# Projections by position block, a resident u D, fewer loads and a new stage order in a fused attention and state-space kernel

## The chip, the cores and the metric

The kernel runs on one core of a Trainium2 chip, in one launch. The metric is the device time of a run in microseconds (us), median of the runs shown. The engines are TensorE (PE; its weight loads, PEld, are listed apart), VectorE (DVE), ScalarE (ACT), GpSimd (POOL) and SyncE (SP); SPq, ACTq, POOLq are their sequencers, which issue DMAs. A profile of one execution shows what each engine did and what it waited for.

## The reference

Two unrelated layers of one sequence of 2048 positions and 640 channels each, side by side in the output:

```python
# part A: sliding local dilated attention; H = 32, Dh = 20, W = 8, dil = 2
qkv = (x @ wqkv).reshape(B, S, 3, H, Dh)            # q, k, v by head
idx = pos[:, None] - 2 * arange(8)[None, :]         # 8 keys: 0, 2, .., 14 positions back
logits = einsum("bhsd,bhswd->bhsw", q, k[idx]) * Dh ** -0.5    # below position 0: -1e9
o = einsum("bhsw,bhswd->bhsd", softmax(logits), v[idx])
a = o @ wo
# part B: a diagonal state-space layer as a long convolution; N = 192
dt = exp(log_dt);  l = arange(2048) rounded to bf16
K = einsum("dn,dnl,dn->dl", C, exp(dt * A * l), dt * B).real   # A, B, C complex, 640 x 192
y = irfft(rfft(pad(u)) * rfft(pad(K)))[:L] + u * Dskip
out = concatenate([a, y], -1)                        # [1, 2048, 1280], bf16
```

## The kernel before, in words

**Part B** works through the channels in five chunks (`NCH` = 5, 128 channels each, c = 0 to 4). The table of the kernel K comes from powers of exp(dt A): `partB_prep` turns the parameters over with matmuls (`flip`, L175) so that the states lie on partitions; `gens` (L234) makes 11 powers with sines and stores them to DRAM (`Gdram`; chunks 0 and 1 in one batch, `gens0`, chunks 2 to 4 in another, `gens2`). For each chunk `Tables` loads them and builds by complex products on VectorE an X table of 20 entries (`xtab`) and a Y table of 33 entries (`ypos`, `yneg`; L264 to L269 and L313). `kgen` (L335) contracts them over the states on TensorE, in four pieces q of 128 small matmuls (L350, L355); each piece ends with a copy to `Kd` (L357), and a shift of `Kd` by DMA from GpSimd's queue follows (L360). Only one Y table is in memory at a time, and two X tables.

The convolution is a two-stage Fourier transform as matmuls: `spread` (L364) brings K into order, `f1` (L386) is the first stage, for u (`first_u`) or K, `f2` (L397) the second. `swap_halves` (L415) makes a copy with the halves exchanged by DMA, `product` (L420) does the complex product in place with four VectorE multiplications of 128x2048 (L422, L423, twice each), `ia` (L426) is the first stage back and its result Z is stored to DRAM for chunks 0 to 2 (`Zdram`) and kept for 3 and 4 (`Z34`). `inverse` (L787) is the second stage back (`last00` to `last03` for chunks 0 to 2, `last10` to `last13` for 3 and 4, each a quarter of l0). It loads a quarter of `Zdram` as `zq` (one buffer) and of the transposed u as `uq`, multiplies `uq` by Dskip on VectorE (L796), adds it with an identity matmul (L800), adds the transform (L803), and stores 4 pieces (L806).

**Part A** loads x transposed (`load`, 20 transposing DMAs on SP, L453) and projects it, 15 calls of `proj` (L465) over 5 tiles of 128 columns for each of k, q, v: four position blocks of 512 by 5 matmuls of 128x512, with a copy to `st` (two buffers, L472), and one store of 128 rows of 4 KB to DRAM (`qd`, `kd`, `vd`). Then four position blocks b of 512 go through `fetch` (q and k tiles by 10 loads), `logits` (L515: 10 VectorE products of 128x2048, L524, and 40 matmuls, exponential and normalisation, L528 to L542), `fetch_v` (20 loads), `av` (L544: 10 more products, L554, and 160 matmuls, L560) and `out_proj` (L566).

**The order.** Every stage runs under `at(name)`, which sets a priority from the place of that name in the list `ORDER`; a scheduler in the build then picks by it among the instructions that its own time simulation says are ready, and fixes one order for each engine and queue. Apart from that list (L138 to L144) the loop over c in the body says what stands in which pool. The tables' pool is released when the last `kgen` has run, and `HB` (the 4 MB matrix of the last stage, four loads of 1 MB) and `Z34` come in its place. The tail is made of the `last` stages.

Of the kernel before, what the change touches and what calls it, by code (L numbers as in the profile page):

```python
# [10 lines left out]
A = mybir.AluOpType  # L11
# [6 lines left out]
NCH = 5  # L18
# [120 lines left out]
k4 am2 inv4 v0 weights k0 u1 spec2 am0 q3 tab2 tab4 v3 prep load taby2 ypos1 ypos0 out1 xtab2 xtab0 tab1 tab0 q2 q1 swap1 k1 yneg1 load2 v2  # L139
mag2 u0 yneg0 fetch0 v4 q0 spread0 k2 tab3 mag0 kgen2 mag1 gens0 kgen4 last13 q4 fetch1 spec1 inv0 kgen1 kgen0 u2 ypos2 gens2 v1 prod4 taby3  # L140
yneg2 kgen3 k3 taby4 spec3 spec0 taby1 fetch2 ypos3 yneg4 spread3 inv3 logits0 swap0 xtab1 last10 xtab3 u3 inv2 spread1 taby0 u av3 av0
fetchv0 swap2 last12 av2 out0 prod1 inv1 yneg3 prod2 logits3 spec xtab4 mag4 last03 u4 fetchv1 ypos4 last11 last02 last01 swap3 mag3 out3
fetchv3 prod3 spec4 fetchv2 spread2 fetch3 av1 swap4 spread4 prod0 last00 out2 logits1 logits2 hb
# [4 lines left out]
def partB_prep(tc, pools, prm, Gd):  # L148
# [5 lines left out]
    nat = [pp.tile([128, NCH, CW], bf16, name="nat", tag="nat", bufs=5) for _ in range(6)]  # L154
    ldt = pp.tile([128, NCH], bf16, name="ldt")
    lsrc = prm["B_log_dt"].rearrange("(g c t) -> g t c", g=4, c=NCH, t=32)
    eng = [nc.sync, nc.scalar]
    for g in range(4):
        eng[g % 2].dma_start(out=ldt[32 * g:32 * g + 32, :], in_=lsrc[g])
    for a, nm in enumerate(["B_A_re", "B_A_im", "B_C_re", "B_C_im", "B_B_re", "B_B_im"]):  # L160
        src = prm[nm].rearrange("(g c t) n -> g t c n", g=4, c=NCH, t=32)
        for g in range(4):
            (eng[g % 2] if a < 2 else nc.gpsimd).dma_start(out=nat[a][32 * g:32 * g + 32], in_=src[g])
# [11 lines left out]
    def flip(a, diag):  # L175
        psb = [psp.tile([128, 512], f32, name="ps_tr", tag="b", bufs=4) for _ in range(2)]
        for c in range(NCH):
            rhs = dg[:, c, :] if diag else ident[:]
            for h in range(2):
                hs = slice(64 * h, 64 * h + 64)  # L180
                col = c * CW + 64 * h
                nc.tensor.matmul(psb[col // 512][:, col % 512:col % 512 + 64], lhsT=nat[a][:, c, 0:128], rhs=rhs[:, hs], start=True, stop=True, skip_group_check=True)
# [397 lines left out]
def kernel(  # L580
# [71 lines left out]
    with at("prep"):  # L652
        ta, wi, weights = partB_prep(tc, pools, prm, Gd)
# [200 lines left out]
```

## Time and profile before

| what | us |
|---|---|
| median of 3 runs | 465.58 (461.92 to 467.53) |
| the profiled execution's own time | 465.34 |
| its span, first to last instruction | 468.0 |
| TensorE busy | 341.5 |
| VectorE busy | 309.3 |
| ScalarE busy | 260.9 |
| GpSimd busy | 36.7 |

The span is the time from the first to the last instruction of the profiled execution. Busy times are sums over an engine's instructions. The profile's other parts: 40 slices of the span with a digit for the busy share in tenths; the chain of work that ended last, followed back from the last instruction; groups of instructions with their idle time before them and who ended it. A row of a window lists the window, its length, the busy time (and count) of PE, PEld, DVE, ACT and POOL, the granted clock of TensorE, the busy share of the DMA engines and GB/s. A row of waits gives who waited for whom, the sum in us, how often, and the longest.

| product c | first start of L422, us |
|---|---|
| 0 | 206.4 |
| 1 | 272.1 |
| 2 | 327.7 |
| 3 | 382.6 |
| 4 | 411.1 |

### The profile page before, as it was taken

What the parts mean: (1) busy time and instruction counts of PE and PEld (TensorE: products, weight loads), DVE (VectorE), ACT (ScalarE), POOL (GpSimd) and SP (SyncE); (2) the same over time, 40 slices, a digit from 0 to 9 for tenths busy, and PEclk for the clock granted to TensorE, in tenths of its full rate; (3) what the DMA queues carried; (4) which work ended last, traced back from release to release, by engine and by line L of the source; (5) the groups of instructions that cost most, each with busy time, mean ns of one, the idle gap of its engine ahead of it and who ended that gap; (6) DMA issues with size and microseconds to landing.
All of it is one profiled execution on the core that took longest, in us unless ns stands there. A gap on an engine that the chain in (4) does not pass through costs nothing.

```text
span 468.0 us, 13264 instructions
## 1 busy us (share of the span) xinstructions
PE 341.5 (73%) x5672; PEld 214.7 (46%) x5684; DVE 309.3 (66%) x448; ACT 260.9 (56%) x570; POOL 36.7 (8%) x80
## 2 busy tenths in 40 slices
PE   0558986999498783639488657899866789967654
PEld 0223432644146352427354446546454556645453
DVE  0576999987799477999029996099911679392101
ACT  1768543997672396624058743288322986936322
POOL 6830000003000200000020000200001000000000
PEclk9956898989898697666769869579985998989876
DMA  7999999345877684103824206143375934205966
GB/s 236 210 210 192 289 243 272 104 154 171 272 255 255 152 241 112 29 19 77 243 53 124 71 23 178 55 120 85 106 207 166 368 94 121 74 1 158 219 157 110
DMA packets 90378, 72.86 MB, mean 156 GB/s; under 512 B 44528, under 2 KB 82656, under 8 KB 88656
## 3 DMA queue, kind: packets, MB, share of 16 engines
q1 hardware_dynamic: 83920, 64.43, 51.2%
q0 software_dynamic: 2352, 5.18, 4.1%
q10 hardware_dynamic: 4048, 2.41, 2.3%
q8 instruction: 44, 0.72, 0.7%
q14 instruction: 14, 0.11, 0.1%
HBM read 38.93 MB, written 24.71 MB: 136 GB/s over the span
## 4 chain that ended last, share of the span: by engine, by line
PE 38%; DVE 20%; DMA 16%; issue 12%; ACT 8%; SPq 4%; ACTq 0%; DVEq 0%; POOL 0%; POOLq 0%
PE ps_p L471 10%; PE ps_k L355 6%; PE ps_k L350 6%; PE ps_ia L435 4%; DVE prod L524 4%; DVE p L554 4%; DMA Gdram<-cs 4%; DMA zq<-Zdram 3%; PE ps_ib L803 3%; SPq L453 3%; DMA kd<-st 2%; DVE krtmp L265 2%; ACT mag L307 2%; ACT Sp L412 2%; DMA Xg<-Gdram 2%
## 5 line engine op out<-in xcount | busy, mean ns | idle before, releaser
L471 PE MATMUL ps_p<-xT,w 128*128 128x512 bf16 x288 | 80.2, 421 | 24.3 <-ACT st L472 15.8
L471 PEld LDWEIGHTS <-w 128*128 128x128 bf16 x300 | 30.1, 105 | 63.0 <-issue 33.9
L524 DVE TENSOR_TENSOR prod<-qb,kb 128x2048 bf16<-128x2048 bf16 x40 | 47.3, 1217 | 7.1 <-PE ps_l L528 6.0
L472 ACT CAST st<-ps_p 128x512 bf16<-128x512 f32 x60 | 34.2, 585 | 31.7 <-PE ps_p L471 23.3
L554 DVE TENSOR_TENSOR p<-vb,attn 128x2048 bf16<-128x2048 bf16 x40 | 47.1, 1217 | 2.1 <-PE ps_o L560 2.0
L408 PE MATMUL ps_f<-A,cT 64*128 64x128 bf16 (+1 forms) x768 | 36.4, 230 | 16.3 <-ACT Sp L412 8.6
L394 ACT CAST A<-ps_f 128x512 bf16<-128x512 f32 x80 | 42.1, 614 | 8.3 <-PE ps_f L393 8.1
L412 ACT CAST Sp<-ps_f 128x512 bf16<-128x512 f32 (+1 forms) x96 | 42.8, 579 | 6.0 <-PE ps_f L408 5.9
L355 PE MATMUL ps_k<-Ytab,Xtab 64*20 64x33 bf16 x1280 | 28.3, 244 | 20.2 <-issue 20.2
L408 PEld LDWEIGHTS <-cT 64*128 64x128 bf16 x768 | 31.0, 105 | 25.5 <-issue 24.7
L357 ACT CAST Kd<-ps_k 128x264 bf16<-128x264 f32 x20 | 7.5, 379 | 61.7 <-PE ps_k L355 61.7
L796 DVE TENSOR_TENSOR uq<-uq,Dsb 128x1536 bf16<-128x1536 bf16 (+1 forms) x8 | 6.6, 825 | 50.7 <-DMA uq<-Udram 37.4
L560 PE MATMUL ps_o<-p,cHs 64*32 64x256 bf16 x640 | 31.2, 308 | 11.4 <-DVE p L554 10.1
L436 ACT CAST Z<-ps_ia 128x512 bf16<-128x512 f32 x40 | 21.6, 594 | 29.6 <-PE ps_ia L435 29.5
L355 PEld LDWEIGHTS <-Xtab 64*20 64x20 bf16 x1280 | 22.3, 124 | 26.3 <-issue 24.3
L350 PE MATMUL ps_k<-Ytab,Xtab 128*20 128x33 bf16 x1280 | 28.1, 249 | 5.4 <-issue 5.4
L435 PE MATMUL ps_ia<-cE,Sp 128*128 128x128 bf16 x160 | 23.7, 244 | 9.7 <-DVE Sp L423 9.7
L350 PEld LDWEIGHTS <-Xtab 128*20 128x20 bf16 x1280 | 22.6, 128 | 12.8 <-issue 11.2
L573 PE MATMUL ps_op<-wo,oT 128*128 128x320 bf16 x160 | 27.9, 321 | 0.0
L307 ACT ACTIVATE mag<-ta 128x192 bf16<-128x192 f32 x80 | 21.7, 353 | 10.4 <-DVE Ytab L313 10.4
L264 DVE TENSOR_TENSOR Ytab<-Ytab 128x384 bf16<-128x384 bf16 (+2 forms) x15 | 13.3, 888 | 21.4 <-DMA Ytab<-Gdram 21.1
L528 PE MATMUL ps_l<-prod,cGs 128*32 128x512 bf16 x160 | 24.7, 420 | 3.2 <-DVE prod L524 3.0
(101 smaller groups left out, 600.6 us busy)
## 6 DMA issues: line engine op xcount, KB each, us to landing
vb<-vd SPq DMA_DIRECT2D x80, 65.5 KB, 2.3
UT<-Sp SPq DMA_DIRECT2D x10, 512.0 KB, 7.3
HB<-k_HB SPq DMA_DIRECT2D x4, 1024.0 KB, 8.7
Gdram<-cs SPq DMA_DIRECT2D x11, 288.0 KB, 3.2
Xg<-Gdram SPq DMA_DIRECT2D x4, 768.0 KB, 7.1
Zdram<-Z SPq DMA_DIRECT2D x3, 1024.0 KB, 9.5
zq<-Zdram SPq DMA_DIRECT2D x12, 256.0 KB, 4.8
kb<-kd SPq DMA_DIRECT2D x20, 131.5 KB, 2.7
```

Of the source, the lines that this page charges most:

```text
L307: pin(self.nc.scalar.activation(out=self.mg[b // 8][:, b % 8], in_=ta[:, s], func=ACT.Exp, scale=-16.0 * (b + 1)))
L350: MM(o, lhsT=X[:, :, part, col], rhs=Y[:, :, part, col], start=False, stop=False, tile_position=(0, 32 * g), skip_group_check=True)
L355: MM(o, lhsT=X[hb:hb + 64, :, part - 2, col], rhs=Y[hb:hb + 64, :, part - 2, col], start=False, stop=(part == 3), tile_position=(hb, 32 * ...
L394: nc.scalar.copy(out=A1[:].rearrange("p k r s t -> p (k r) s t")[:, :, sig, 8 * q:8 * q + 8], in_=ps[:])
L408: nc.tensor.matmul(ps[h][:, kk], lhsT=C["T"][hs, k, 64 * (1 - r):64 * (1 - r) + 128], rhs=A1[hs, k, r, s0:s1, :].rearrange("p s t -> p (s ...
L412: nc.scalar.copy(out=o, in_=ps[h][:].rearrange("p k (s t) -> p s t k", t=64))
L435: nc.tensor.matmul(ps[:, i], lhsT=X[:, h, 4 * t:4 * t + 4, :].rearrange("p g k -> p (g k)"), rhs=C["E"][:, n_, :], start=(i == 0 and n_ == ...
L471: nc.tensor.matmul(ps[:], lhsT=self.w[which][:, kt, 128 * ct:128 * ct + 128], rhs=self.xT[:, kt, 512 * sc:512 * sc + 512], start=(kt == 0) ...
L472: nc.scalar.copy(out=st[:, sc], in_=ps[:])
L524: V.tensor_tensor(out=pr[:], in0=q[ct][:].unsqueeze(1).to_broadcast([128, 4, PB]), in1=windows(k[ct][:, 8 - 8 * wg:8 - 8 * wg + PB], 2, 4) ...
L554: V.tensor_tensor(out=p2[:], in0=windows(self.v[b][t][:, 2 * qp:2 * qp + 2, 0:PH], 2, 4), in1=at[:].unsqueeze(2).to_broadcast([128, 4, 2, ...
L560: nc.tensor.matmul(ps[half][32 * q:32 * q + 32, t % 2], lhsT=C["Hs"][r], rhs=p2[r, m, q2, :], start=(t % 2 == 0 and m == 0), stop=(m == 3) ...
```

## The change

- **Start.** The parameters are loaded with the channel as j p (128 partitions in a run) by one DMA each, all on SP, in an order written out; so are the w matrices and the Gdram stores of `gens0`, which were on the ScalarE and GpSimd queues. The flips then need 32-column pieces: 240 matmuls in place of 120. Five transposes of x are in the list of loads, and the other 15 are issued behind the stores of the powers (`then`, two or one behind each). Buffers of cs: 6 for 4, of nat: 6 for 5.
- **Projections.** `proj(which, sc)` does one position block of 512 for all five column tiles; the store has 128 partitions of five pieces of 1 KB. The 12 calls are ordered by block. q and k share one DRAM tensor `qkd`, so that `fetch` needs 5 loads of 128x2x526 a block in place of 10.
- **Loads of v.** Two tiles of 8 and 12 rows in place of five of 4: 8 loads a block in place of 20.
- **kgen in pieces.** The four pieces have four names in the order.
- **u D resident.** The whole transposed u is loaded once (2.5 MB, one DMA of SP) behind the last kgen, multiplied by Dskip in five VectorE multiplications, and kept. HB's loads move to GpSimd's queue.
- **Tail.** Chunks 0 to 2 go in eighths of l0, with two half buffers for z: 32 stores of 32x8x96 in place of 16 of 32x16x96, 24 loads of 128 KB in place of 12 of 256 KB.
- **A new `ORDER`** with the new names.

```diff
-    for a, nm in enumerate(["B_A_re", "B_A_im", "B_C_re", "B_C_im", "B_B_re", "B_B_im"]):
-        src = prm[nm].rearrange("(g c t) n -> g t c n", g=4, c=NCH, t=32)
-        for g in range(4):
-            (eng[g % 2] if a < 2 else nc.gpsimd).dma_start(out=nat[a][32 * g:32 * g + 32], in_=src[g])
+        def par(nm, t):
+            nc.sync.dma_start(out=t[:], in_=prm[nm].rearrange("(j p) n -> p j n", p=128))
...
+        for m in range(4 * NCH):
+            g, c, j, r = m // NCH, m % NCH, m // 4, slice(32 * (m % 4), 32 * (m % 4) + 32)
+            rhs = (dg[:, j, :] if diag else ident[:])[:, r]
+            for n0, n1, p, col in ((0, 128, slice(0, 128), c * CW + 32 * g), (128, 192, slice(64 * (g // 2), 64 * (g // 2) + 64), c * CW + 128 + 32 * (g % 2))):
+                nc.tensor.matmul(psb[col // 512][p, col % 512:col % 512 + 32], lhsT=nat[a][:, j, n0:n1], rhs=rhs, start=True, stop=True,
+                                 tile_position=(0, p.start), skip_group_check=True)
...
-        (nc.sync if ca else nc.scalar).dma_start(out=Gd[...], in_=cs.rearrange("p c r n -> p c (r n)"))
+        o = nc.sync.dma_start(out=Gd[...], in_=cs.rearrange("p c r n -> p c (r n)"))
+        then(o)
...
+    def then(store):
+        with at("load"):
+            for _ in range(2 if len(xs) > 8 else 1):
+                if xs:
+                    ins = a.load_x(xs.pop(0))
+                    tc.add_manual_dep(ins.ins, store.ins.name, ..., reason="order of the transfers")
...
-    def proj(self, which, ct):
-        st = self.pools["xw"].tile([128, 4, 512], bf16, name="st", tag="st", bufs=2)
-        for sc in range(4):
+    def proj(self, which, sc):
+        st = self.pools["xw"].tile([128, 5, 512], bf16, name="st", tag="st", bufs=2)
+        for ct in range(5):
...
+            nc.sync.dma_start(out=self.qkd[:, :, "qk".index(which), s], in_=st[:])
...
+            t = p.tile([128, 2, HALO + PB], bf16, name="qk", tag="qk", bufs=3)
+            nc.sync.dma_start(out=t[:], in_=self.qkd[:, ct, :, i0:i0 + PB + HALO])
...
+        for i, (d0, n) in enumerate(((0, 8), (8, 12))):
+            v = p.tile([128, n, PH + 6], bf16, name="vb", tag=f"vb{i}", bufs=1)
...
+        for q in range(4):
+            with at(f"kgen{self.c}{q}"):
+                self.kgen_part(q, Kd)
...
-            nc.sync.dma_start(out=HB[...], in_=hsrc[:, 16 * q:16 * q + 16])
+            nc.gpsimd.dma_start(out=HB[...], in_=hsrc[:, 16 * q:16 * q + 16])
+    with at("ud"):
+        nc.sync.dma_start(out=uD[:].rearrange("p x l t -> p (x l t)"), in_=Ud[:].rearrange("p x l t -> p (x l t)"))
+    for x in range(0, 2 * NCH, 2):
+        with at(f"ud{x // 2}"):
+            dv = ...
+            V.tensor_tensor(out=uD[:, x:x + 2], in0=uD[:, x:x + 2], in1=dv, op=A.mult)
...
+    zb = fp.tile([128, 128, 32], ..., tag="Z")[...].rearrange("p (b c x t) -> p b c x t", b=2, c=3, t=32)
+    for e in range(8):
+        with at(f"last0{e}"):
+            for i in range(3):
+                nc.sync.dma_start(out=zb[:, e % 2, i], in_=Zd[i][:, 16 * e:16 * e + 16])
+            inverse([0, 1, 2], zb[:, e % 2], 8 * e, 8)
```

In the order that the build fixes, the two kernels differ as follows. Before, stage c of the loop held the tables of chunk c + 2 and part A's block c, and the four pieces of a kgen stood together on TensorE; in the changed kernel the logits of block c + 1 stand beside kgen of chunk c + 2 (pieces 0 and 1 together, pieces 2 and 3 among the logits' matmuls, first_u and spread), and block c + 1's av and out_proj lie one stage earlier. 235 projection matmuls stand before kgen 0. Table 4 stands wholly ahead of product 2 on VectorE, and the five multiplications of uD ahead of av 3's last three products and product 3. After ia of chunk 4 only the last stages are left.

## The prediction

> **What bounds the kernel now.** I read the first page of the profile, the chain that ended last, the waits, and the busy time by windows, in this order. The page first:
>
> ```profile
> PE 341.5 (73%) x5672; PEld 214.7 (46%) x5684; DVE 309.3 (66%) x448; ACT 260.9 (56%) x570; POOL 36.7 (8%) x80
> ...
> DMA  7999999345877684103824206143375934205966
> ...
> PE 38%; DVE 20%; DMA 16%; issue 12%; ACT 8%; SPq 4%; ACTq 0%; DVEq 0%; POOL 0%; POOLq 0%
> ```
>
> No engine is the bound: TensorE has the most work and is free for 27% of the span, and the chain changes engines. DMA is full at both ends only. So I look for the stretch in which each wait stands. The chain in order of time (start, length, what):
>
> ```profile
> 70.28 6.09 DMA kd<-st
> ...
> 231.25 3.23 issue
> ...
> 426.20 5.46 DMA zq<-Zdram
> ...
> 442.26 5.20 DMA zq<-Zdram
> ...
> 453.47 3.24 DMA uq<-Udram
> ```
>
> Early, a projection waits for the store of an older one; in the middle, TensorE has pauses that nothing in the trace explains but which lie in kgen; at the end, every quarter waits for its zq load, then for uq. The waits give the sizes:
>
> ```profile
> DVE uq L796 <- DMA uq<-Udram: 37.4, 6, 19.4
> ...
> DVE Ytab L264 <- DMA Ytab<-Gdram: 21.1, 3, 15.6
> ...
> PE ps_k L355 <- issue: 20.2, 9, 4.0
> ...
> DVE Xtab L264 <- PE ps_k L355: 16.3, 1, 16.3
> ```
>
> Uq, Ytab and Xtab are one story: VectorE stands still for 16.3, 15.6 and 19.4 us while kgen 2, 3 and 4 run, because nothing else is in its order. The windows (TensorE, its weight load, VectorE, ScalarE busy):
>
> ```profile
> 213.00:278.00 65.00, 46.56 (x911) 32.76 (x912) 43.80 (x62) 34.70 (x80) 2.63 (x6) 0.79 0.36 102
> 278.00:338.50 60.50, 52.19 (x1039) 34.87 (x1037) 44.52 (x54) 32.62 (x66) 2.62 (x6) 0.82 0.37 102
> ...
> 420.40:468.00 47.60, 29.97 (x400) 22.62 (x400) 8.03 (x9) 18.38 (x40) 0.00 (x0) 0.81 0.70 158
> ```
>
> In the two cycle windows neither engine is full; in the last, TensorE has 30.0 us of work in 47.6.
>
> **The measure of the sum.** The first multiplication of product c (L422) starts at 206.4, 272.1, 327.7, 382.6 and 411.1 us, and the span ends at 468.0. I price the change stretch by stretch between these marks, by the order of instructions in both kernels. The profiled execution took 465.34 us, 2.7 less than its span, and the median of three was 465.58: the sum is made in the span, and 2.7 is taken off.
>
> **Start to product 0 (206.4 us).** SP takes over what ScalarE's and GpSimd's queues issued: parameter loads (28 issues, 22 of them elsewhere; now 7), three w loads and the 11 Gdram stores of gens0, beside its 20 transposes. One transpose holds SP for 1.26 us (L453), so 20 are 25 us, between 5.0 and 39.4 us of the span; now 15 of them are tied one or two behind each Gdram store of gens0, so that late transposes hold later stores and late stores hold transposes. It costs nothing as long as TensorE has an earlier position block to project. The flips double from 120 to 240 matmuls: 120 more at the 0.105 us from one start to the next that the trace shows for those of L182 and L186, +12.6 us of TensorE. They lie in the first 60 us, where TensorE was busy 3.5 of 17 and 21.2 of 31 us; but gens0's last steps now stand on VectorE behind the Gt products, which wait for the last two flips, and table 0's X chain comes some 13 us later by this. TensorE's own order decides instead: 235 projection matmuls stand before kgen0. 25 of them take 5.95 us at full clock (48 took 11.40), one group is through at 48 us as before, 8.4 more end at 98; kgen0 started at 86.1 and now at 98, with only two groups (11.9 us) left to interleave, and ends at 117 against 111.7. Xg(0)'s load stands on SP behind the last Gdram store, the last u loads and a v store; X(0) has until 98. Then Ytab(1) (3 us to land), ypos 8.4 and yneg 4.5 on VectorE, kgen1 from about 140 to 160 (before 138.3 to 157.4), logits 0 mixed into it to 165, normalisation to 170. From there VectorE has 30.5 us to product 0 (attn 1.1, av 11.4, the next table's X 15, 3 of waits), where it took 34.4 with a wait of 7.6 for the Xg load, which is now issued before it is needed. 200.5: **-6**, from -14 (VectorE never waits) to 0 (the 13 us late table is felt to the full, less the 13 us of interleaving that it saves).
>
> The stores of a projection become 640 packets of 1 KB in place of 128 of 4 KB. The trace's mean packet of 1 KB takes 57 ns and of 4 KB 181 ns: 2.3 us of 16 engines in place of 1.4. Landing was 2.7 to 6.8 us; I take 6 or less, where two buffers of st and 6 us of a group just hide it. No gain excluded: 0 to +25, kept for a rival.
>
> On one queue for all loads the Trainium skill has a rule: "DMA: Bandwidth & Descriptors", section "Issuing engines are not separate DMA queues", says that issuing from several engines saves just the sequencer's time, usually small beside the transfer. By that rule the move would be free; by the trace's transposes SP holds 25 us, which my sum hides behind projections either way.
>
> **Product 0 to product 1 (65.7 us).** Here kgen2 used to leave VectorE idle for 16.3 us; now logits 1 stand beside it. TensorE had 46.6 us of work in the window of 65, now about the same and the pauses of 6.6 us (3.33 and 3.23 in the chain) with some 4 of waits at the norm: 57. VectorE's own share is 47.1 us. **-8.7**, from -13 to -5.
>
> **Product 1 to product 2 (55.6 us).** The new order lays table 4 wholly before product 2. VectorE's rows add up to 59.6 us in this stretch (logits 11.4, attn 1.1, av 11.4, product 4.6, one table 28 and a part of the next), more than the whole stretch took. With one wait for the norm of about 5 us (L542 waited 12.5 us in 2) it is 64.5: **+8.9**, from +6 to +14. VectorE is the bound here, and nothing hides it.
>
> **Product 2 to product 3 (54.9 us).** VectorE has 37.4 us, TensorE the 52.2 of the cycle window and the pauses of kgen4 (3.99 and 3.28 us in the trace): 59. New is a wait: the five uD multiplications (1.14 us each) stand on VectorE before av 3's last three products and product 3, and behind them waits TensorE for av 3 and ia 3. uD (2.6 MB) and HB (4.2 MB) start together when kgen4 frees the tables; at the 368 GB/s of the page's slice with HB they take 18.5 us, and VectorE gets there some 16 us after kgen4: 2 us more. In all 60.6: **+5.7**, from +2 to +11. The shift of Kd(4) stands on POOL's queue behind the four HB issues; spread 4 is late by it only if the issues block, and the trace's four HB issues all stand at 360.5.
>
> **Product 3 to product 4 (28.5 us).** Block 3 of part A is done earlier. TensorE was busy 26.6 of 31.4 us in this window; with av 3 out of it (31.2 us of L560 by four: 7.8) and out_proj 3 in its place (27.9 by four: 7.0), about 25.5: **-3**, from -8 to 0.
>
> **Product 4 to the end (56.9 us).** The products of 4.6 and ia4 (8 us) stay. The three zq groups of the chain cost 6.5, 6.2 and 6.1 us from issue to the last landing, 18.8 together, on the path because zq has one buffer; uq's is 3.2. Now eighths have two buffers, the first two loaded before ia4, uD is resident. A half load of 128 KB in 1 KB packets takes 3 x 128 x 57 ns / 16 = 1.4 us of the engines and lands in about 3; TensorE needs 3.7 us for an eighth. So 22 us leave the path; what takes their place is SP: the out stores rise from 32 to 48, each some 0.45 us (4 took 2.4 for 256 KB before, now smaller), and 15 of them stand before the loads of eighths 6 and 7. SP: 48 x 0.45 + 18 x 0.5 = 31 us. With TensorE's 30 us and the last landing of 3 us: 36 to 40 after ia4's start. I take 48 for the whole stretch: **-8.9**, from -13 to -4.
>
> **Sum.** -6 - 8.7 + 8.9 + 5.7 - 3 - 8.9 = -12.0: a span of 456.0, a time of **453** (-2.7%). The bounds, partly independent, give 443 to 462.
>
> **Where a rule speaks on the pauses.** The 3 to 4 us pauses of kgen coincide with packets on the queue named instruction (44 of 16 KB), so they look like code loading, and I keep them in all cycles. The Trainium skill, "Runtime: NRT & Kernel Launch", section "Instruction fetch mechanics", has blocks of 16 KiB too and calls the crossing mostly hidden. By the rule the pauses would be something else, and the sum would be about 7 us lower for each kgen from which they go.
>
> **The rivals.**
> - *No measurable change.* VectorE loses both stretches at their worst end, 70 and 66 us: +11, 464. For it: 59.6 us of rows leave no slack for a late norm, and VectorE waited 12.5 us at L542. Against it: product 2 needs table 4 only because it was put there.
> - *More gain.* Interleaving hides the pauses of the pieces 2 and 3 (3.3 in each of three kgen: -9.9), and the waits of the norm vanish (-6): 437. For it: logits and u are TensorE work between the pieces. Against it: a pause stops the whole engine, whatever stands next.
> - *Slower: the projection stores.* Place: PE's projections before kgen0, waiting for st. Price: with two buffers a group takes (6 + L)/2 once a landing L exceeds 6 us, so nine groups cost 4.5 x (L - 6). The gain of 12.6 is gone at L = 8.8, slower by 2% begins at L = 10.9, and L = 12 gives 480. For it: kd's stores on the chain took 5.29 and 6.09 us with DMA at 0.95 of its time, the new ones have 1.25 times the bytes in five times the packets, and the first 48 us are full of DMA (0.89 to 1.04). Against it: q and v landed in 2.8 to 6.8.
> - *The flips move nothing:* if the parameter loads are late, +3 us, inside the ranges.
>
> **How the numbers follow.** Forecast 0.50, no change 0.20, more gain 0.12, slower 0.18. About 2% is what a measurement of this kernel can tell from no change: faster means below 456.3, slower above 474.9. Of the forecast's own range 443 to 462 some seven tenths lie below 456.3 (0.36), with 0.12 of the second rival and a little of the first: faster 0.50. Same: 0.13 of the forecast and 0.16 of the first rival, 0.29. Slower: 0.18 and the upper tails, 0.21. The range reaches to 433 for the second rival and to 477 for half of the third.
>
> **What would show it.** Right: no zq-like wait in the tail; products 1 and 2 more than 60 us apart with VectorE busy nearly all of it; products 0 and 1 under 60 apart, with no VectorE idle beside kgen2; kgen0 near 98 us. Wrong: st waits of ScalarE for its stores over 3 us a group; a wait of VectorE for uD above 6 us; product 0 after 210; ib matmuls waiting for zb; pauses longer than 7 us in a kgen.

## The result and the profile after

The changed kernel takes 480.43 us (478.44 to 484.06 in 4 runs) against 465.5 for the kernel before: a ratio of 1.034, with a 95% interval of 1.024 to 1.043. It is slower; 453.0 had been forecast, and the range ended at 477. The profiled execution took 478.44 us, with a span of 476.5. The two times given for the kernel before don't belong together: the record lists a span of 463.6 us and a granted clock of 0.86 for the execution of 465.34 us, and the trace has a span of 468.0 and a clock of 0.83, so it is likely that of another, slower execution. In every execution whose span is listed, the time lies 1.7 to 2.2 us above the span. The spans of the two traces differ by 8.5 us, the medians by 14.9: the table of stretches below leaves some 6 us of the loss out.

The page of the changed kernel, the lines that answer to those of before (busy times; DMA in 40 slices; the chain, which here reaches back only to 285 us):

```profile
PE 365.8 (77%) x5794; PEld 233.6 (49%) x5804; DVE 307.4 (65%) x445; ACT 263.0 (55%) x570; POOL 27.2 (6%) x65
...
DMA  9995687963189974743543448323067195502556
...
PE 15%; DVE 7%; DMA 7%; issue 4%; SPq 4%; ACT 2%; ACTq 0%; POOL 0%; DVEq 0%; POOLq 0%
```

TensorE has 24.3 us more work than before (365.8 for 341.5) with only 122 instructions more. The waits of the whole span (who, for whom, sum in us, times, longest):

```profile
ACT ysb L822 <- DMA out_dram<-ysb: 26.2, 10, 10.3
...
PE ps_k L348 <- issue: 12.2, 6, 3.3
...
PE ps_ib L818 <- ACT ysb L822: 11.2, 5, 6.6
...
DVE Xtab L252 <- DMA Xg<-Gdram: 6.1, 4, 2.9
...
DVE Ytab L252 <- DMA Ytab<-Gdram: 4.5, 2, 3.9
...
PE ps_ib L821 <- DMA zb<-Zdram: 3.4, 4, 1.6
```

The waits that the change was aimed at did shrink: those of VectorE for Ytab (21.1 before), for Xtab behind kgen (16.3) and for uq (37.4) are gone or small, the pauses of kgen are 15.6 us (12.2, and 3.4 at L353) for 25.6 (20.2, and 5.4 at L350), and the tail waits 3.4 us for z. So the time went elsewhere. By the marks (first start of the product's multiplication, us):

| stretch | before | predicted | after | prediction missed by |
|---|---|---|---|---|
| start to product 0 | 206.4 | 200.5 | 219.1 | +18.6 |
| 0 to 1 | 65.7 | 57 | 55.4 | -1.6 |
| 1 to 2 | 55.6 | 64.5 | 67.8 | +3.3 |
| 2 to 3 | 54.9 | 60.6 | 57.9 | -2.7 |
| 3 to 4 | 28.5 | 25.5 | 24.3 | -1.2 |
| 4 to end | 56.9 | 48 | 52.0 | +4.0 |

The windows of these stretches from product 0 on (length, then busy PE, PEld, DVE, ACT, POOL):

```profile
219.00:274.40 55.40, 50.30 (x984) 32.78 (x984) 48.05 (x68) 32.62 (x72) 2.62 (x6) 0.86 0.43 121
274.40:342.30 67.90, 50.28 (x1036) 32.59 (x1036) 60.97 (x79) 37.08 (x84) 2.62 (x6) 0.78 0.38 99
342.30:400.20 57.90, 50.45 (x1009) 33.56 (x1011) 37.67 (x34) 32.08 (x66) 4.43 (x8) 0.88 0.62 206
...
424.50:476.50 52.00, 24.81 (x344) 19.83 (x344) 4.63 (x4) 15.87 (x34) 0.00 (x0) 0.70 0.46 97
```

In the second of them VectorE is busy 61.0 of 67.9 us: the bound that the new order sets there. The large miss is the start. Its windows:

```profile
0.00:17.00 17.00, 8.63 (x57) 6.55 (x57) 1.83 (x7) 4.48 (x9) 9.30 (x22) 1.00 1.04 213
17.00:48.00 31.00, 29.71 (x161) 18.61 (x163) 13.29 (x31) 15.71 (x31) 0.00 (x0) 0.75 0.91 211
...
126.00:158.00 32.00, 18.91 (x187) 8.38 (x180) 31.39 (x54) 24.00 (x47) 5.00 (x10) 0.77 0.81 246
```

From 17 to 48 us TensorE is full, 29.7 of 31, where it was busy 21.2 before, and VectorE does 13.3 us of work where it did 22.5. The same window of the kernel before:

```profile
17.00:48.00 31.00, 21.19 (x117) 9.48 (x118) 22.50 (x49) 23.25 (x54) 10.26 (x17) 0.66 1.04 199
```

What fills TensorE is in its timeline (start, length, instructions in a row):

```profile
8.37 12.33 PE L173 MATMUL ps_tr<-dg,nat 128*128 128x32 bf16 x80 [8.37 <-DVE dg L165]
24.87 5.54 PE L173 MATMUL ps_tr<-cident,nat 128*128 128x32 bf16 x40
35.26 5.53 PE L173 MATMUL ps_tr<-cident,nat 128*128 128x32 bf16 x40
42.83 12.36 PE L173 MATMUL ps_tr<-dg,nat 128*128 128x32 bf16 x80
```

These are the flips: 35.8 us in all. The same six flips took 12.3 us before. VectorE waits for them, in the waits of the start (0 to 219 us):

```profile
DVE uc L728 <- DMA us<-in_B_u_dram: 17.1, 3, 7.0
DVE pr L199 <- PE ps_tr L173: 15.0, 1, 15.0
...
PE ps_k L341 <- DVE Ytab L301: 12.6, 1, 12.6
DVE wk L184 <- PE ps_tr L173: 11.1, 1, 11.1
...
PE ps_p L465 <- ACT st L466: 9.3, 6, 4.5
```

and stands in the middle of its order, with the powers of `gens0` (L236) half done and the Gt products (L199) ahead of the rest. VectorE's timeline:

```profile
32.79 0.55 DVE L236 SCALAR_TENSOR_TENSOR ab<-ph 128x384 f32<-128x384 int32 x1
...
48.38 0.69 DVE L199 TENSOR_TENSOR pr<-ps_tr,cc 128x512 f32<-128x512 f32 x1 [15.04 <-PE ps_tr L173]
...
54.52 0.69 DVE L200 TENSOR_TENSOR pr<-ps_tr,cc 128x512 f32<-128x512 f32 x1 [5.44 <-PE ps_tr L173]
```

So the last power is ready late (68.2 us; 42.7 before), and its store and then the load of Xg(0) leave late. SP's timeline:

```profile
70.49 0.36 SPq L239 DMA_DIRECT2D Gdram<-cs  x1
70.92 1.16 SPq L445 DMA_TRANSPOSE xT<-in_A_x_dram  x1
72.14 1.63 SPq L726 DMA_DIRECT2D us<-in_B_u_dram  x3
75.18 0.38 SPq L469 DMA_DIRECT2D vd<-st  x1
75.66 0.47 SPq L276 DMA_DIRECT2D Xg<-Gdram  x1
```

The last power landed at 73.0 us (before: 49.4), Xg(0) at 81.0 (53.6), table 0 was ready at 112.8 (85.1), kgen0 started at 115.2 (86.1). But TensorE doesn't wait for the table. It goes from its last projection straight into kgen0:

```profile
96.17 15.88 PE L465 MATMUL ps_p<-xT,w 128*128 128x512 bf16 x64 [2.00 <-ACT st L466]
113.06 2.32 PE L465 MATMUL ps_p<-xT,w 128*128 128x512 bf16 x9 [1.02 <-ACT st L466]
115.21 0.40 PE L341 MATMUL ps_k<-Ytab,zw 128*128 128x264 bf16 x2
```

From the end of the flips at 55.2 us these 60.0 us are 52.0 of projections and 7.6 of waits for st. So two chains reach kgen0 2.4 us apart, the table and the projections, and the flips stand ahead of both. The new order wins back 16.4 us between kgen0 and product 0 (103.9 us for 120.3), so the 29.1 us by which kgen0 is late are 12.7 at product 0.

The tail's chain in order of time (start, length, what) is SP itself for long stretches:

```profile
451.32 0.41 SPq L830
...
451.77 0.43 SPq L830
...
460.30 3.48 DMA out_dram<-ysb
```

Here one issue follows the other by 0.45 us, loads of z (L830) and stores of the output (L824) in one line.

### The profile page after: what moved, and what is told of

It reads as the page before. It is cut to its first block, busy times and chain, and to the rows that moved or that the text cites. A ratio compares the mean times of both kernels' runs of the same rounds, so it can differ in the third digit from the quotient of the medians.

```text
span 476.5 us, 13396 instructions
## 1 busy us (share of the span) xinstructions
PE 365.8 (77%) x5794; PEld 233.6 (49%) x5804; DVE 307.4 (65%) x445; ACT 263.0 (55%) x570; POOL 27.2 (6%) x65
## 5 line engine op out<-in xcount | busy, mean ns | idle before, releaser
L512 DVE TENSOR_TENSOR prod<-qk 128x2048 bf16<-128x2048 bf16 x40 | 47.4, 1220 | 12.7 <-PE ps_l L516 10.2
L348 PE MATMUL ps_k<-Ytab,Xtab 128*20 128x33 bf16 x1280 | 36.1, 248 | 12.2 <-issue 12.2
L348 PEld LDWEIGHTS <-Xtab 128*20 128x20 bf16 x1280 | 26.9, 129 | 23.0 <-issue 21.1
L173 PEld LDWEIGHTS <-nat 128*128 128x128 bf16 x240 | 27.2, 113 | 18.6 <-DMA nat<-in_B_A_re_dram 8.4
L402 PEld LDWEIGHTS <-cT 64*128 64x128 bf16 x768 | 28.6, 99 | 13.4 <-issue 11.3
L516 PE MATMUL ps_l<-prod,cGs 128*32 128x512 bf16 x160 | 26.5, 448 | 9.0 <-DVE prod L512 8.9
L353 PE MATMUL ps_k<-Ytab,Xtab 64*20 64x33 bf16 x1280 | 29.9, 244 | 3.4 <-issue 3.4
L561 PE MATMUL ps_op<-wo,oT 128*128 128x320 bf16 x160 | 30.6, 346 | 1.2 <-ACT oT L552 1.2
L173 PE MATMUL ps_tr<-dg,nat 128*128 128x32 bf16 (+1 forms) x160 | 24.7, 222 | 8.4 <-DVE dg L165 8.4
L353 PEld LDWEIGHTS <-Xtab 64*20 64x20 bf16 x1280 | 22.8, 124 | 11.5 <-issue 9.4
L548 PEld LDWEIGHTS <-cHs 64*32 64x32 bf16 x640 | 15.7, 98 | 23.1 <-issue 12.3
L252 DVE TENSOR_TENSOR Xtab<-Xtab,Xg 128x768 bf16<-128x768 bf16 (+2 forms) x35 | 24.5, 700 | 3.4 <-DMA Xg<-Gdram 2.9
```

The source lines that it names most:

```text
L173: nc.tensor.matmul(psb[col // 512][p, col % 512:col % 512 + 32], lhsT=nat[a][:, j, n0:n1], rhs=rhs, start=True, stop=True, tile_position=( ...
L348: MM(o, lhsT=X[:, :, part, col], rhs=Y[:, :, part, col], start=False, stop=False, tile_position=(0, 32 * g), skip_group_check=True)
L353: MM(o, lhsT=X[hb:hb + 64, :, part - 2, col], rhs=Y[hb:hb + 64, :, part - 2, col], start=False, stop=(part == 3), tile_position=(hb, 32 * ...
L402: nc.tensor.matmul(ps[h][:, kk], lhsT=C["T"][hs, k, 64 * (1 - r):64 * (1 - r) + 128], rhs=A1[hs, k, r, s0:s1, :].rearrange("p s t -> p (s ...
L512: V.tensor_tensor(out=pr[:], in0=self.qk[b][ct][:, 0, HALO:].unsqueeze(1).to_broadcast([128, 4, PB]), in1=windows(self.qk[b][ct][:, 1, 8 - ...
L548: nc.tensor.matmul(ps[half][32 * q:32 * q + 32, t % 2], lhsT=C["Hs"][r], rhs=p2[r, m, q2, :], start=(t % 2 == 0 and m == 0), stop=(m == 3) ...
```

## The experiments

Ratios are to the kernel before, run beside each (its medians 465.1 to 467.5 us), with 95% intervals. "e5" and so on name the kernels by their numbers below; times in the start are of the profiled executions.

### The flips

**e2: the new parameter layout and its 240 flips alone, in the kernel before.**

```diff
-        for g in range(4):
-            (eng[g % 2] if a < 2 else nc.gpsimd).dma_start(out=nat[a][32 * g:32 * g + 32], in_=src[g])
+        (eng[a] if a < 2 else nc.gpsimd).dma_start(out=nat[a][:], in_=prm[nm].rearrange("(j p) n -> p j n", p=128))
...
+        for m in range(4 * NCH):   # the flips of the changed kernel
```

> The kernel before with the new parameter layout alone: one load an array on the queues that it had, 240 flip matmuls of 32 columns. Theory F: TensorE gets 20 us more work in the first 60 us, of which it had some 15 us free: product 0 6 to 12 us later, time 471 to 477. If the flips are covered, as predicted: 463 to 468. Rival S and rival P: no change either, 463 to 468.

Measured: 497.69 us, 1.063 [1.058, 1.069]. Product 0 starts at 230.9 us, 24.5 later than before, and the flips take 36.6 us, 24.3 longer. The time is far above that of theory F (471 to 477). The edit isn't alone: the build laid its orders anew, with 190 projection matmuls ahead of kgen0 in its trace for 156 in that of the kernel before, and products 2 and 3 are 62.4 us apart for 54.9. So it shows that nothing covers the longer flips, and not their price to the microsecond. The granted clock isn't what makes them long: in the changed kernel the first 80 flip matmuls took 12.33 us at a clock of 1.00, and the last 80 took 12.36 us at 0.50.

**e5: the changed kernel with neighbouring pieces of a flip merged.** The same loads; pieces of 32 columns that lie side by side go through one matmul with a strided output, 22 a flip for 40.

```diff
-        for m in range(4 * NCH):
+        for j in range(NCH):
+            for n0, n1, first in ((0, 128, 2), (128, 192, 1)):
...
+                    out = bass.AP(out.tensor, out.offset, [list(out.ap[0]), [CW, k], [1, 32]])
+                    rhs = (...)[:, 32 * i0:32 * (i0 + k)].rearrange("p (k t) -> p k t", k=k)
```

> The changed kernel with the same loads and the same positions of the turned parameters, but neighbouring 32-column pieces that land in one run of the target with a stride of 192 put into one matmul: 22 matmuls a flip instead of 40. The order on SP and VectorE stays nearly the same, and 235 projection matmuls still stand before kgen 0. Theory F (TensorE's own flip work, 32.7 us in the profile at 0.134 us a matmul, sets the start): 6 x 18 x 0.134 = 14.5 us less, the flips end near 41 instead of 55 us, kgen 0 near 101 to 106 instead of 115, product 0 at 204 to 210 instead of 219, time 465 to 472. Rival Q (SP's loads and the stores of the powers set it, the flips only wait for data): kgen 0 stays after 110, time 477 to 482.

Measured: 464.17 us (10 runs), 0.998 [0.994, 1.003]: 16.3 us less than the changed kernel, and level with the kernel before. The flips take 12.5 us, Xg(0) lands at 74.4, kgen0 starts at 104.9, product 0 at 209.6, both as theory F said. Its window shows TensorE free again:

```profile
17.00:48.00 31.00, 24.08 (x147) 11.92 (x146) 19.16 (x43) 18.49 (x36) 0.00 (x0) 1.00 0.97 226
```

**e1: the changed kernel with the old layout,** four loads for each parameter and 120 flips.

```diff
-            nc.sync.dma_start(out=t[:], in_=prm[nm].rearrange("(j p) n -> p j n", p=128))
+            for g in range(4):
+                nc.sync.dma_start(out=t[32 * g:32 * g + 32], in_=prm[nm].rearrange("(g c t) n -> g t c n", g=4, c=NCH, t=32)[g])
```

> The changed kernel with the parameters loaded and turned over as before (120 flip matmuls of 64 columns, four loads an array, all on SP); all else as changed. The scheduler then by itself puts the Gt products behind gens0 on VectorE, and 200 projection matmuls instead of 235 before kgen 0. Theory F (the longer flips: six of 5.5 us in the profile, 2.1 us before, fill TensorE from 8 to 55 us, and the Gt products that wait for the last two hold VectorE for 20 us): the projections restart near 45 instead of 55.5 us, product 0 comes at 200 to 206 instead of 219, and the time is 461 to 468. Rival P (the number of projections before kgen 0 sets it): only 35 x 0.24 = 8 us come back, 470 to 474. Rival S (the 1 KB stores hold the projections): no change, 478 to 482.

Measured: 512.1 us, 1.094 [1.087, 1.100]. A miss, and no test: 20 more issues went onto SP's line, other loads were laid ahead of them, and a flip waited 33.3 us for its parameter. It shows only that 28 parameter loads on SP's line come late.

**Why a flip matmul is dear.** 40 matmuls in 5.5 us are 0.138 each, 80 in 12.3 are 0.154. The prediction took 0.105, the mean of the kernel before. But that mean was of two kinds of gaps, and the timeline of the kernel before shows both:

```profile
11.15 0.29 PE L182 MATMUL ps_tr<-dg,nat 128*128 128x64 bf16 x2 [11.15 <-DMA nat<-in_B_A_re_dram]
11.37 0.26 PE L186 MATMUL ps_tr<-dg,nat 64*64 64x64 bf16 x2
11.56 0.29 PE L182 MATMUL ps_tr<-dg,nat 128*128 128x64 bf16 x2
```

Two matmuls of 128x128 weights start 0.05 us apart, two of 64x64 weights together; from one shape of weights to the other it takes 0.17 to 0.19 us. In the changed kernel 128x128 and 128x64 weights stand in turn, so that every matmul is a change of shape, and the starts are 0.14 and 0.17 us apart by turns.

**e15: the changed kernel with the same 240 matmuls, in each flip the 20 of one shape first and then the 20 of the other.**

```diff
-        for m in range(4 * NCH):
-            ...
-            for n0, n1, p, col in (...):
+        for part in range(2):
+            for m in range(4 * NCH):
+                ...
+                n0, n1, p, col = (...)[part]
```

> The changed kernel with its 240 flip matmuls, but in each flip the 20 of weights 128x128 first and then the 20 of weights 128x64, where the changed kernel takes them in turn. In its trace the starts of two neighbours stand 0.14 and 0.17 us apart by turns (clock granted 1.00), while in the kernel with merged pieces two matmuls of one weight shape in a row stand 0.03 to 0.08 apart and only a change of shape 0.14 to 0.18. Theory S (the change of weight shape is the price): a flip of 40 takes about 2.5 to 3.5 us in place of 5.5 to 6.2, the six about 15 to 21 in place of 35.7, the table chain comes earlier as with merged pieces, and the time is 464 to 469. Rival N (the price is the number of loads and matmuls, 240, whatever their order): a flip stays at 5.5 us or more, and the time at 478 to 484.

Measured: ratio 1.020 [1.015, 1.026], from three executions of 472.4 to 475.9 us; 464 to 469 had been forecast. The profiled one took 573.4 us and isn't in the ratio, so the same kernel was run once more for a trace.

> The kernel with 240 flip matmuls and the shapes apart once more, for a trace of its usual course, since it took some 473 us with flips of 9.5 us in all, where the merged pieces gave 464 with 12.6. Theory P (the scheduler lays the order for flips as long as it thinks them, and the number of matmuls has not changed): VectorE's and TensorE's orders ahead of kgen0 are those of the changed kernel, so kgen0 starts 3 to 9 us ahead of its 115.2, at 106 to 112, and the rest of the stretches are as there. Rival L (something later was lost): kgen0 at 105 or before, and a stretch behind product 0 is 5 us or more longer than in the changed kernel (55.4, 67.8, 58.0, 24.3, 52.0).

Measured: 477.59 us in its one execution (the kernel before beside it 467.43). TensorE's timeline:

```profile
9.38 2.90 PE L174 MATMUL ps_tr<-dg,nat 128*128 128x32 bf16 x64 [0.21 <-DVE dg L165]
25.47 1.34 PE L174 MATMUL ps_tr<-cident,nat 128*128 128x32 bf16 x40
28.91 1.29 PE L174 MATMUL ps_tr<-cident,nat 128*128 128x32 bf16 x40
31.22 2.52 PE L174 MATMUL ps_tr<-dg,nat 128*128 128x32 bf16 x80
```

With the 0.65 us of the first 16, 240 matmuls take 8.7 us in place of 35.8. The number is the same, the tiles and the columns are the same, only the order is another: the price is the change of shape (35.8 - 8.7 = 27.1 us for some 230 changes, 0.12 each). Two rivals fall with it. In the first half of a flip four neighbours in a row share their weights, and the step to other weights of the same shape takes 0.03 us like the steps between them. And the step from one 128x64 tile to the one beside it, once in the second half of each flip, takes 0.01 us from start to start. The Trainium skill has this as a rule, in "TensorEngine Tiling (Array Packing)", section "Key Properties": changing the tiling mode, and not just the tile, drains TensorE. These traces agree with it, and give it a size; that a drain is the cause no trace here shows. The prediction didn't weigh it.

But the time didn't follow: kgen0 starts at 110.2 us, 5.0 ahead of the changed kernel, product 0 at 214.8, 4.3 ahead, and from product 1 to product 3 it takes 131.1 us for 125.7. The start gained the 3 to 9 us of theory P, but not for its reason: the orders are not those of the changed kernel (VectorE's differ from about the 50th instruction on, SP's from about the 46th DMA, both ahead of kgen0). In this trace the last power is ready at 47.2 us and its store is issued at 63.4; TensorE waits 19.6 us for st between the flips and kgen0; and VectorE stands 5.2 us in the middle of table 0, where the next table's Xg comes first in its order.

So 27 us less of flips brought the ratio from 1.034 to 1.020, while e5, with flips 4 us longer than here, reached 0.998. What e5 gains beyond e15 can't be the flips' own time. The orders that the build lays for 132 matmuls differ from those for 240, which makes them the likely place, but no run takes this apart.

**e16: e5 with the shapes apart.**

```diff
-        for j in range(NCH):
-            for n0, n1, first in ((0, 128, 2), (128, 192, 1)):
+        for n0, n1, first in ((0, 128, 2), (128, 192, 1)):
+            for j in range(NCH):
```

> The kernel with merged pieces (22 matmuls a flip), with the 11 of weights 128x128 first and the 11 of 128x64 behind them. Theory S: a flip takes about 1.4 to 1.8 us in place of 2.1, 2 to 4 us less in all; product 0 follows Xg(0), whose store stands in SP's line, so the time moves by 0 to -3: 461 to 465. Rival N: 2.1 us a flip, and the time is that of the merged pieces, 464 (462 to 466).

Measured: 466.07 us (10 runs), 1.001 [0.997, 1.006]. The flips take 6.2 us for e5's 12.5, Xg(0) lands at 73.0 for 74.4, kgen0 starts at 102.4 for 104.9, product 0 at 206.8 for 209.6, and the time is the same within its uncertainty. So from 12.5 us down the flips bring little; something else holds Xg(0) at 73 us.

### What else holds the start

In every trace but that of e15's long execution kgen0 starts 0.1 to 3.1 us behind the moment when table 0 is ready, and table 0 is ready 27 to 33 us behind the landing of Xg(0) (51 in e1). Yet TensorE waits for the table in e9 alone (1.8 us); in every other trace it comes straight from a projection. So the table and the projections arrive together, and the traces don't say which would have come first without the other. The runs below ask what makes Xg(0) late.

**e4: the weights' part of the preparation behind `gens0` in the list** (the name `weights` moved behind `gens0`).

> The changed kernel with one name moved in its order list: the stage weights (flips 2 to 5 and the Gt products) stands behind gens0. The flips stay as long as they are, but are interleaved with projections, and the Gt products come behind gens0's steps on VectorE, which then do not wait 20 us. If the VectorE stall is what costs the start (theory F's second half): product 0 at 206 to 211, time 466 to 473. If it is TensorE's 20 us of extra flips alone: kgen 0 stays at 115 and the time within 2 us of the changed kernel, 478 to 482.

Measured: 483.59 us, 1.035 [1.032, 1.039]. The Gt products no longer hold the powers on VectorE, and another wait stands in their place:

```profile
DVE ph L235 <- ACT cs L237: 24.2, 4, 17.9
```

the sines on ScalarE, late behind its copies. Kgen0 starts at 119.3, 4 us later.

**e9: e5 with three buffers for st** (cs 5 for 6 and nat 5 for 6, to fit).

> The kernel with few flips, and three buffers for the projections' st instead of two (paid for by one buffer less for cs and for nat). In its profile of few flips TensorE waits 16.8 us for st, whose stores stand on SP's queue behind powers, transposes and u loads and land 4.7 to 5.8 us after their issue. The scheduler now lays 305 instead of 235 projection matmuls before kgen 0. Theory W (the stores' way through SP's queue is the next bound of the start): the waits of TensorE for st fall under 5 us, the last projection ends before 125 us instead of 135.6, time 456 to 461. Rival V (VectorE's tables are the bound: kgen 1 waits 12.6 us for Ytab whatever TensorE does): the projections end earlier, kgen 1 starts at 146 to 150 as before, time 462 to 467.

Measured: 479.33 us, 1.032 [1.025, 1.039]. Both expectations missed: with a third buffer the scheduler laid all 300 projection matmuls ahead of kgen0. The last one ends at 111.4 us, in time by theory W, but Xg(0) lands at 86.5 and kgen0 starts at 113.2.

**e10: e5 with the copies of u (uc) on GpSimd; e11: e9 and e10 together.**

```diff
-            V.tensor_copy(out=uc[:], in_=us[:].rearrange("p l (x t) -> p x l t", t=16))
+            nc.gpsimd.tensor_copy(out=uc[:], in_=us[:].rearrange("p l (x t) -> p x l t", t=16))
```

> The kernel with few flips, and the four copies uc<-us on GpSimd instead of VectorE, so that VectorE never stands before a u load that has not landed (17.2 us in 2 waits with few flips). Theory V (VectorE, in order, is what the tables of the start wait for): Ytab of chunk 1 is ready 8 to 15 us earlier, kgen 1 starts at 133 to 141, product 0 at 195 to 202 instead of 209.6, time 451 to 458. Theory W (TensorE's projections and their stores): within 3 us of the kernel with few flips, 461 to 467.

> Both edits on the kernel with few flips: three st buffers and uc on GpSimd. If TensorE's stores and VectorE's u waits bind one after the other, only this gives the whole: product 0 at 192 to 200, time 448 to 456. If only one of them counts, it is no better than the better of the two single edits.

Measured: e10 467.55 us, 1.005 [1.000, 1.009], with Xg(0) at 69.5 and kgen0 at 102.1, 2.8 us earlier than in e5, all lost again by product 0 (213.6); e11 479.28, 1.030 [1.022, 1.038]. No gain.

**e12: e5 with the stores of the powers on ScalarE's queue,** the transposes tied behind w_v's load instead. **e13: e12, and the Gt products tied behind the last power on VectorE.**

```diff
-        o = nc.sync.dma_start(out=Gd[...], in_=cs.rearrange("p c r n -> p c (r n)"))
+        o = (nc.sync if ca else nc.scalar).dma_start(out=Gd[...], in_=cs.rearrange("p c r n -> p c (r n)"))
...
+                f = V.tensor_tensor(out=pr[0], in0=b0, in1=cc[:, c0, s], op=A.mult)
+                tc.add_manual_dep(f.ins, pools["last_cs"].ins.name, ...)   # e13 alone
```

> The kernel with few flips, and the Gdram stores of gens0 on ScalarE's queue as before the change; the 15 later transposes of x are tied behind the last weight load on SP instead of behind those stores. In the profiles the last gens0 store landed at 49.4 us before the change, at 73.0 after it and Xg of table 0 at 53.6 against 81.0; the table needs 31 us from there. Theory G (SP, which holds powers, transposes, u loads and projection stores in one line, makes table 0 late): Xg(0) lands 5 to 12 us earlier than the 74.4 of few flips, kgen 0 starts at 94 to 100 instead of 104.9, time 452 to 460. Rival D (VectorE's order makes it late, the Gt products that wait for the flips stand ahead of the last powers): Xg(0) lands after 70, time within 3 us of few flips, 461 to 467.

> As the kernel with few flips and the stores on ScalarE's queue, and the Gt products tied behind the last power of gens0 on VectorE, which is the order of the kernel before. Theory D (VectorE's order): the last gens0 store lands near 50 us, Xg(0) at 56 to 63, kgen 0 starts at 90 to 96, time 450 to 458, and clearly less than with the stores moved alone. Theory G: no more than the stores moved alone. If kgen 0 comes earlier in either run and kgen 1 still starts at 146 to 150, the second batch of powers and table 1 on VectorE hold the start, and the time stays at 461 to 467.

Measured: 482.82 us, 1.039 [1.033, 1.045], and 483.68, 1.039 [1.033, 1.044]. In e12 the stores no longer wait (the last power is ready at 60.4 us and its store issued at 60.6), but this power comes 9.4 us later than in e5, Xg(0)'s load is issued on SP only at 70.7, and Xg(0) lands at 77.1, no earlier. Far behind the start a wait appears that the prediction had named as a risk, the shift of Kd(4) behind HB on GpSimd's queue; products 3 and 4 are 46.8 us apart for e5's 25.0, which is more than e12's whole loss:

```profile
PE ps_s L383 <- DMA Kd<-Kd: 23.3, 1, 23.3
```

In e13 Xg(0) lands at 69.5 and kgen0 starts at 100.9, but product 0 at 228.7; why wasn't found.

**e14: e5 with all the powers ahead of the Gt products,** on VectorE (as in e13) and on ScalarE (the copies cc behind the last sine).

> The kernel with few flips, its stores of powers on SP as there, and both the Gt products on VectorE and the copies of flips 2 and 3 on ScalarE tied behind the last power of gens0. In the run with the stores on ScalarE and only VectorE's order restored, the powers still stopped from 37 to 48 us, as ScalarE stood at copies of flips and projections. If the two in-order engines together are what makes the powers late: the last gens0 store lands by 58 us (66.7 with few flips), Xg(0) by 66 (74.4), table 0 is ready by 95 (102.6) and kgen 0 starts at 94 to 100, time 455 to 461. If SP's line is the rest of it, the powers are ready early and their stores still land after 65: time 461 to 467. If the last flips, now later behind the copies, hold table 0 instead (it starts from the Gt product), no gain or a loss: 464 to 472.

Measured: 467.61 us, 1.004 [0.998, 1.010]. The last power is ready at 45.6 us; its store is issued at 60.6. SP's timeline:

```profile
60.58 1.08 SPq L250 DMA_DIRECT2D Gdram<-cs  x1
61.72 1.17 SPq L456 DMA_TRANSPOSE xT<-in_A_x_dram  x1
63.00 0.51 SPq L217 DMA_DIRECT2D Gdram<-Gt  x1
63.55 2.37 SPq L737 DMA_DIRECT2D us<-in_B_u_dram  x4
66.03 0.69 SPq L217 DMA_DIRECT2D Gdram<-Gt  x1
66.82 0.45 SPq L480 DMA_DIRECT2D vd<-st  x1
67.32 0.76 SPq L287 DMA_DIRECT2D Xg<-Gdram  x1
```

A finished power stands 15.0 us in SP's line, behind 17 DMAs that are issued one right after the other from 44.9 us on, and Xg(0)'s load leaves 6.7 us behind the store. The other traces with short flips show the same: the last power is ready at 51.0 us in e5 and its store issued at 64.2, at 49.7 and 62.6 in e16. In the changed kernel itself it waited 2.3 us (68.2 and 70.5); there the flips made the power late. So in the kernels with short flips the last power comes 17 to 23 us earlier, and SP's line takes 11 to 14 of them back.

The rule that the prediction weighed, "DMA: Bandwidth & Descriptors", section "Issuing engines are not separate DMA queues" of the Trainium skill, calls the sequencer's time usually small beside the DMA. One by one that holds here (these issues take 0.4 to 2.0 us and land after 2.6 to 5.5); in one line they add up to 15 us. Whether a start with SP's line relieved would be faster stays open: e12 and e13 took the stores off it, and their powers came later than e5's.

### The tail and the middle

**e3: two of the four output stores of a piece on GpSimd's queue.**

```diff
-            nc.sync.dma_start(out=dst_b[...], in_=ysb[32 * g:32 * g + 32])
+            (nc.sync if g % 2 else nc.gpsimd).dma_start(out=dst_b[...], in_=ysb[32 * g:32 * g + 32])
```

> The changed kernel with half of the last stages' out stores (two of four per piece) on GpSimd's queue instead of SP's. Theory T (the tail is set by SP, which issues 48 stores and 18 loads one after the other at 0.45 us from 441 to 470 us, and TensorE waits 11 us for ysb): 6 to 10 us off the last stretch, 470 to 475. Rival: the landing of the stores and TensorE set it: within 2 us, 478 to 482.

Measured: 478.66 us, 1.025 [1.017, 1.032]; product 4 to the end 51.3 us for 52.0. The rival held: ScalarE still waits 22.6 us for places of ysb, 26.2 in the changed kernel.

**e7: eight places for ysb** in a dead tile. **e8: the same in e5.**

```diff
-        ysb = ip.tile([128, 1024], bf16, name="ysb", tag="ysb", bufs=2)[:, 0:nl * 32 * n]...
+        slot = slots.pop(0)
+        ysb = yb[:, slot:slot + nl * 32 * n]...
```

> The changed kernel with eight places for ysb in a dead tile instead of two buffers, so that no copy of the last stages waits for an older store to land; stores and their queue are the same. Theory L (ScalarE's 26 us of waits for the landing of out stores hold TensorE in the tail): 5 to 8 us off the last stretch, 472 to 476. Theory T (SP issues 48 stores and 18 loads one after the other, 29 us): the end is set by the last issue, within 3 us, 477 to 482; the profile then shows SP issuing without a pause to the end.

> Both edits together, few flips and eight places for ysb. If the two losses are independent, their gains add: by theories F and L 459 to 466, which would be level with the kernel before or 1% under it; by rival Q and theory T 474 to 482.

Measured: 481.55 us, 1.036 [1.027, 1.044], tail 51.6; e8 465.88, 0.998 [0.992, 1.004], no better than e5. In e7 the waits for ysb are gone and the loads of z are late instead:

```profile
PE ps_ib L822 <- DMA zb<-Zdram: 9.8, 3, 6.9
```

SP issues a DMA every 0.5 us to 475 us, with few pauses (the longest 3 us), as theory T said. More buffers don't help the tail; neither do two queues for the stores with two buffers. The two together weren't tried.

**e6: table 4's Y part tied behind product 2,** to take the VectorE-bound stretch apart.

```diff
-            Kds[c + 2] = make(c + 2)
+            Kds[c + 2] = make(c + 2, done=done if c == 2 else None)
```

> The changed kernel with one ordering edge more: table 4's Y part stands on VectorE behind product 2. If VectorE is the bound from product 1 to product 3 (it was busy 61.0 of 67.9 us, and 37.7 of 57.9): product 2 comes 8 to 13 us earlier and product 3 at the same time, as the work is only moved: the time stays within 3 us of the changed kernel, 477 to 484. Rival (the place of table 4 is a loss by itself, since products 1 to 2 took 55.6 us before): 5 to 10 us less, 470 to 476.

Measured: 490.31 us, 1.054 [1.047, 1.062]. Both expectations were wrong: products 1 and 2 come 59.3 us apart for 67.8, but 2 and 3 80.3 for 57.9, since a later kgen4 frees the tables' pool later, and uD's load stands behind that:

```profile
DVE uD L815 <- DMA uD<-Udram: 29.5, 1, 29.5
```

So table 4 ahead of product 2 costs 8.5 us there, near the 8.9 of the prediction, and in this kernel its place behind product 2 costs more.

## Why the prediction was wrong, step by step

- **The flips (the term that failed).** "120 more at the 0.105 us", +12.6 us, covered by an idle TensorE. They cost 23.5 more (35.8 for 12.3). 0.105 was the mean over pairs; the change turned pairs into singles, and each then costs 0.14 to 0.15. And the cover was counted on TensorE's idle time of before (9.8 of 31 us), which 23.5 us overfill.
- **"TensorE's own order decides instead", kgen0 at 98.** In the trace TensorE does come to kgen0 by its own order, but at 115.2. The sum let the last 8.4 groups begin at 48 us; the flips end at 55.2 (7.2 us). It gave these groups 50 us; they took 60.0, with 52.0 of work and 7.6 of waits for st, which the sum put at nothing. Table 0 was ready at 112.8, so an earlier TensorE would have waited for it. The prediction saw that chain ("some 13 us later") and let it go because X(0) "has until 98". From kgen0 to product 0 it was right: 103.9 us for 102.5.
- **SP's line "costs nothing".** Nearly so in the changed kernel, where the last power waited 2.3 us in it and the flips hid the rest. With short flips it waits 12.9 to 16.2 us there (e5, e14, e16, e17), and Xg(0) stays at 73.0 to 75.5 us. Of the 18.6 us by which the start was missed, e5 took back 9.5 and e16 12.3. No run took SP's line away, so its share of the rest stays open.
- **kgen1** waited 12.6 us for Ytab, with VectorE busy 31.4 of 32 us. It does so in e5 too (12.6), where table 0 comes 9.6 us earlier; the sum has no such wait, but kgen0 to product 0 came out right without it.
- **The middle was right:** 57, 64.5, 60.6 and 25.5 against 55.4, 67.8, 57.9 and 24.3. VectorE bound the second stretch as said; uD, priced at a wait of 2 us, landed 0.4 us before VectorE came to it.
- **The tail** was 4 us too cheap. The waits for zq did go; in their place SP's issues (0.45 to 0.6 us apart, near the 0.45 to 0.5 estimated, with pauses of up to 1.6 between) and ysb made 52.0 for 48.
- **From span to time** the sum took 2.7 us off, a difference of two executions, as said above. The time is 1.9 us above the span after, as it is by 1.7 to 2.2 everywhere else. That is worth 4.6 us of the miss; 2.0 more lie between this execution and the median (480.43).
- **The slower rival, 480, named the right time for a wrong reason.** The stores of a projection land in 5.6 us (median), below the 6 that it needed exceeded, and TensorE waits 9.3 us in 6 for st where it waited 15.8 before.
- **The pauses** fell from 25.6 us to 15.6, part of what the second rival had hoped for.

The stretches add up: 18.6 - 1.6 + 3.3 - 2.7 - 1.2 + 4.0 is 20.4 of span, with 4.6 and 2.0 the 27 us between 453 and 480.

## What to carry to other kernels

Price a matmul from the gaps between neighbours of the same and of another weight shape, never from the mean of a line: order all pieces of one shape together, and merge what lies side by side. Where several engines with fixed orders hand on a short early chain (here parameter, flip, power, store, table), follow that chain through every queue before trusting the idle time of the engine with the most work. An edit in a kernel whose orders come from a scheduler is rarely alone: e4, e6 and e13 changed what they aimed at and lost it elsewhere in a newly laid order, and e5 gained more than its shorter flips explain. Check that a time and a span come from the same execution before adding one to the other.

## What the runs showed of the hardware

- From one matmul of 32 or 64 columns to the next, a change between 128x128 and 128x64 weights (or 64x64) takes 0.10 to 0.19 us from start to start; without a change it is 0.00 to 0.08. 240 small matmuls took 35.8 us in one order (the changed kernel) and 8.7 in another (e17).
- In e14 SP took 1.2 to 2.0 us to issue a transposing DMA and 0.4 to 1.1 for a plain one; with 17 of them in a row ahead of it, a store that was ready waited 15.0 us.
- The length of a flip didn't follow the granted clock: 80 matmuls with a change at each took 12.33 us at 1.00 and 12.36 us at 0.50, both in the changed kernel.
